# A fused adaLN layer on one core: GpSimd keeps only short operations, the modulation weights come in other tiles, and all engines get a new order

## The chip, the cores and the metric

The kernel runs on one core of a Trainium2 chip. The metric is the device time of one execution in microseconds (us). Five engines work side by side: PE (TensorE, matrix products), DVE (VectorE), ACT (ScalarE), POOL (GpSimd) and SP (SyncE, which here only issues transfers). Each engine runs its own list of instructions strictly in order, and waits for others through semaphores. Transfers are issued by SP and by ACT. What they share are 16 DMA engines.

## The reference, cut to what matters

```python
mod = (silu(c) @ w_mod).reshape(1, 6, 1, 448)   # sa, ca, ga, sb, cb, gb
h = layernorm(x) * (1 + ca) + sa                # x: 2048 x 448
x = x + ga * (attention(h @ wqkv) @ wo)         # 16 heads of 28; each row sees 8 rows, 2 apart
h = layernorm(x) * (1 + cb) + sb
x = x + gb * (silu(h @ w1) @ w2)                # 448 -> 1792 -> 448
```

Inputs and output are bf16.

## The kernel before, in words

The 2048 rows are split by parity (a row attends only rows of its own parity), which leaves 1024 positions of two rows each. Four chunks of 256 positions are normalized and projected; the attention runs over nine units of 2 x 57 positions, the feed-forward over four chunks again.

A chunk of the first half goes through these steps. **Load** of x (`ldx`). **Normalization**: statistics on DVE (`st`, L356 to L358), the inverse root on POOL (`rstd`, L372), the scaled rows `xn` on DVE (L387) or ACT (L385). **Transpose**: for chunk 0 on PE (L446), for the others by a DMA transpose that SP issues (L404). **Modulation**: scale and shift by columns of `modc` (`mod`, L238 on DVE, L236 on ACT). **Projection** to q and k on PE (`qk`, L473, four pairs of 14 matmuls a chunk) and, by unit, to v (L490). A unit then has logits (`lg`, L528), two exponentials on ACT (`ex`, L535), a mask product on DVE (`mk`, L586), the product with v (`av`, L602), the division on DVE (`rc` and `on`, L609 and L614), a DMA transpose back (`otr`, L617) and a copy to its place (`al`, L623). The output projection (`wo`, L653) follows, then the residual (`res`, L661) and the second normalization, and the feed-forward: L682, silu on ACT (L687), L707 and, for the last rows, L719.

The gates ga and gb are multiplied into the weights wo and w2 (`wog`, L782; `w2g`, L784), once they have been computed on PE (`ga`, `gb`, L335) from the modulation weights `wmod`. `wmod` shares its tile, `both`, with the hidden layer. The columns of sa, ca, sb and cb come from 32 small matmuls each (L317, `mod1`, `mod2`). Before any of it, PE runs matmuls on a tile of zeros (L293, "junk"), and the qk weights are spread out to 32 columns a head on their way to the tile `wp` (`pad`, L432).

Most PE work comes in **pairs**: a first half (`.S`), and a second half (`.C`) that may begin only when POOL, in its own order, has run an empty instruction that waits for the first (`signal`, L218). So whatever stands ahead of that instruction on POOL holds up PE.

Nothing is scheduled at run time. The table `ORDER` lists all 640 steps by number with a letter for the engine (p PE, a ACT, v DVE, g POOL, s SP); each engine's list is what the table has for it. The four double banks of PSUM (`ps`) and the other buffers are handed out in the same order. Each transfer, whoever issues it, takes one of eight completion semaphores in turn (DMAHW0 to 7), and waits until the transfer that had it before has landed.

## Time and profile before

| | |
|---|---|
| median of 3 runs | 189.6 us (187.68 to 190.51) |
| profiled execution, its own time | 186.92 us |
| its span, first to last instruction | 185.1 us |
| mean granted TensorE clock in it | 0.979 of full speed |
| busy: PE, DVE, ACT, POOL | 162.3, 93.7, 96.2, 44.7 us |
| first matmul of the qk projection that is followed by the others without a stop | 14.65 us |
| first matmul of the second chunk pair's projection (chunk 2) | 45.66 us |
| first feed-forward matmul | 81.75 us |
| last matmul of the feed-forward | ends at 176.46 us |

An engine that is busy for its whole span bounds the kernel; one that is not may still hold up another that waits for a certain instruction of it. So the span is read in stretches, and within a stretch by what PE waited for.

### The profile page before, as it was taken

To read this page: it belongs to the slowest core of one execution; us is meant where nothing else is said; L and a number is where in the kernel's file an instruction comes from. 1 tells how busy PE (TensorE), PEld (TensorE's weight loads), DVE (VectorE), ACT (ScalarE), POOL (GpSimd) and SP (SyncE) were. 2 spreads that over 40 slices of the span, in tenths; PEclk is the share of its full clock that TensorE was granted. 3 is DMA by queue.
4 is the path that set the end of the run, shared out by engine and by line. 5 is a ranking of instruction groups with operands and counts; after the bars stand their busy time and mean duration, and the time that the engine had idled before them with its cause. 6 is when DMAs were issued, how large, how long until landed. Compare 5 with 4: busy or idle time off the path is not lost.

```text
span 185.1 us, 6152 instructions
## 1 busy us (share of the span) xinstructions
PE 162.3 (88%) x2713; PEld 84.8 (46%) x2713; DVE 93.7 (51%) x194; ACT 96.2 (52%) x128; POOL 44.7 (24%) x91
## 2 busy tenths in 40 slices
PE   7979799677868989879999999999999999999910
PEld 2344354354334545545556644455444445554700
DVE  2879999679557858993327484032062000002620
ACT  2140598725259657586698785585338854200000
POOL 6346434551100059432304202000400000000000
PEclk9999999997899999999999999999999999999995
DMA  5993599999687956434003343900009000000132
GB/s 176 339 360 84 96 200 239 110 132 119 210 62 197 212 199 31 89 75 102 0 0 60 64 104 68 109 0 4 0 3 259 4 0 4 0 0 4 50 102 66
DMA packets 33114, 18.20 MB, mean 98 GB/s; under 512 B 25016, under 2 KB 32568, under 8 KB 33080
## 3 DMA queue, kind: packets, MB, share of 16 engines
q1 hardware_dynamic: 30752, 14.92, 40.7%
q10 hardware_dynamic: 2328, 2.81, 4.9%
q8 instruction: 23, 0.38, 0.9%
q14 instruction: 11, 0.09, 0.2%
HBM read 9.86 MB, written 1.84 MB: 63 GB/s over the span
## 4 chain that ended last, share of the span: by engine, by line
PE 70%; DVE 8%; DMA 6%; POOL 5%; ACT 3%; issue 2%; DVEq 0%; POOLq 0%; ACTq 0%
PE ps L682 23%; PE ps L707 20%; PE ps L473 10%; PE ps L653 5%; DMA wqk<-in_A_wqkv_dram 4%; PE ps L490 4%; PE ps L719 3%; PE ps L602 2%; PE ps L528 2%; POOL rs L372 2%; DMA x_all<-in_A_x_dram 2%; DVE xn L387 1%; ACT ho L236 1%; DVE st L356 1%; DVE p L586 1%
## 5 line engine op out<-in xcount | busy, mean ns | idle before, releaser
L707 PE MATMUL ps<-w,both 64*128 64x448 bf16 x392 | 38.9, 349 | 0.0
L687 ACT ACTIVATE both<-ps 128x1024 bf16<-128x1024 f32 x28 | 27.8, 1022 | 17.6 <-PE ps L682 17.2
L473 PE MATMUL ps<-ho,wp 64*128 64x512 bf16 x224 | 26.9, 385 | 3.9 <-POOL ho L623 1.4
L682 PEld LDWEIGHTS <-w 64*128 64x128 bf16 x392 | 20.0, 94 | 22.5 <-issue 1.0
L707 PEld LDWEIGHTS <-both 64*128 64x128 bf16 x392 | 19.0, 94 | 17.6
L682 PE MATMUL ps<-h,w 64*128 64x512 bf16 x196 | 22.5, 376 | 0.6 <-ACT v L495 0.6
L682 PE MATMUL ps<-wqk,w 64*128 64x512 bf16 x196 | 22.3, 376 | 0.0
L661 DVE SCALAR_TENSOR_TENSOR x_all<-ps,x_all 128x448 bf16<-128x448 f32 x16 | 9.3, 621 | 22.6 <-PE ps L653 22.6
L473 PEld LDWEIGHTS <-wp 64*128 64x128 bf16 x224 | 11.3, 95 | 17.3 <-issue 3.8
L535 ACT ACTIVATE p<-ps 128x912 bf16<-128x912 f32 x18 | 15.9, 929 | 5.4 <-PE ps L528 5.3
L742 DVE TENSOR_TENSOR wqk<-ps,x_all 128x896 bf16<-128x896 f32 x3 | 3.3, 1087 | 26.8 <-issue 26.8
L490 PE MATMUL ps<-wv,ho 64*64 64x448 bf16 x252 | 14.8, 352 | 1.8 <-issue 1.4
L477 ACT CAST qk<-ps 128x1024 bf16<-128x1024 f32 x11 | 10.5, 1016 | 7.9 <-PE ps L473 7.9
L387 DVE TENSOR_SCALAR xn<-x_all,mv,rs 128x512 bf16<-128x512 bf16 x26 | 12.4, 509 | 4.2 <-POOL rs L372 4.2
L364 POOL TENSOR_SCALAR mv<-sums 128x2 f32<-128x2 f32 x8 | 3.0, 376 | 41.8 <-DVE x_all L661 34.3
L653 PE MATMUL ps<-wo,ho 64*128 64x448 bf16 x112 | 12.8, 350 | 0.0
L367 ACT ACTIVATE scr<-x_all,mv 128x448 bf16<-128x448 bf16 x16 | 10.6, 664 | 3.8 <-POOL mv L364 3.5
L586 DVE TENSOR_TENSOR p<-p,maskb 128x1824 bf16<-128x1824 bf16 x9 | 11.7, 1299 | 1.7 <-ACT p L535 1.7
L356 DVE BATCH_NORM_STATS2 st<-x_all 128x6 f32<-128x448 bf16 x16 | 9.9, 619 | 2.7 <-DMA x_all<-in_A_x_dram 2.7
L614 DVE TENSOR_TENSOR o<-ps,rc 121x896 bf16<-121x896 f32 x9 | 9.8, 1086 | 0.7 <-DMA op<-o 0.5
L490 PEld LDWEIGHTS <-ho 64*64 64x64 bf16 x252 | 7.1, 106 | 6.5 <-issue 4.0
L293 PE MATMUL ps<-junk 64*128 64x512 bf16 x56 | 9.0, 488 | 1.2 <-DVE junk L203 1.2
(84 smaller groups left out, 175.7 us busy)
## 6 DMA issues: line engine op xcount, KB each, us to landing
w<-in_B_w_dram SPq DMA_DIRECT2D x2, 896.0 KB, 6.0
w<-in_B_w_dram SPq DMA_DIRECT2D x2, 784.0 KB, 5.9
x_all<-in_A_x_dram SPq DMA_DIRECT2D x2, 448.0 KB, 10.0
out_dram<-ot SPq DMA_DIRECT2D x4, 224.0 KB, 2.2
both<-in_w_mod_dram ACTq DMA_DIRECT2D x1, 784.0 KB, 8.5
wo<-in_A_wo_dram SPq DMA_DIRECT2D x2, 392.0 KB, 6.0
both<-in_w_mod_dram SPq DMA_DIRECT2D x1, 784.0 KB, 9.3
out_dram<-wqk SPq DMA_DIRECT2D x3, 224.0 KB, 2.3
```

What stands on the lines that cost most here:

```text
L356: V.bn_stats(out=st[:], in_=x_all[:, us[t], :])
L367: S.activation(out=scr[:], in_=x_all[:, us[t], :], func=ACTF.Square, bias=mv[:, t, 0:1], accum_out=mv[:, t, 1:2])
L387: (V if o["eng"] == "dve" else G).tensor_scalar(out=out_, in0=in_, scalar1=mv[:, t, 0:1], scalar2=rs[:, t:t + 1], op0=ALU.subtract if b el ...
L473: return [matmul(t[:, j, :], lhsT=w, rhs=hT[rows, :, kt, s0:s0 + CP], start=start, stop=stop)]
L477: copy_on(o)(out=qk[:, :, g, :, s0:s0 + CP], in_=t[:].rearrange("p j (t s) -> p j t s", t=2))
L490: return [matmul(t[half(par), j, 0:D], lhsT=hT[rows, par, kt, k0:k0 + KB], rhs=wv[rows, kt, :], start=start, stop=stop) for par in range(2)]
L535: S.activation(out=p_of[u][:, 2 * t * w:2 * t * w + 2 * w].rearrange("p (j n) -> p j n", j=2), in_=bank(a, t)[:, :, 0:w], func=ACTF.Exp, s ...
L586: V.tensor_tensor(out=p, in0=p, in1=m, op=ALU.mult)
L653: x = matmul(t[:, par, 0:D], lhsT=oT[rows, par, i // 2, 128 * m:128 * m + 128], rhs=wo[rows, j, :], start=(j == 0), stop=(j == 5))
L682: return [matmul(t[:, i // 7, :], lhsT=w1[rows, kt, 128 * i:128 * i + 128], rhs=h[rows, :, kt, :], start=start, stop=stop)]
L687: S.activation(out=hid[:, k % 2, :, i, :], in_=t[:], func=ACTF.Silu)
L707: x = matmul(t[:, par, 0:D], lhsT=hid[half(hf), k % 2, jj, ii, 128 * j:128 * j + 128], rhs=w2[half(hf), ii + 7 * jj, :], start=(way == 0 a ...
```

## The change

It does five things. (1) Modulation weights: the 448 rows of `w_mod` were four tiles of 112 rows; they are now rows 0, 128, 256 in steps of 128 plus a fourth tile at row 320 that overlaps the third by 64 rows. The entries of silu(c) that belong to the doubled rows are left at zero in one of the two (L303 after, four small matmuls instead of one). Each load becomes two (three tiles, then one). (2) The vectors ga, sb, cb and gb, which were three loads, are one pair of loads. (3) Long POOL work goes elsewhere: two of the four pads, the first gate product on wo, four of the seven on w2 and two alignment copies now may run on DVE (or ACT) only. What stays on POOL is the inverse root, a few 128x2 operations, the fills and the signals. (4) Adding epsilon moves from DVE (16 instructions, L358) into the POOL step of the inverse root (one more 128x2 instruction for eight pairs); `nm`, needed only where ACT normalizes, is left out elsewhere, and `nm` and `mean` may run on DVE as one instruction. (5) `ORDER` is new throughout. By kind, the moves between DVE and ACT are: normalizations on DVE 26 to 20 and on ACT 6 to 12, modulations on DVE 14 to 19 and on ACT 14 to 9, evictions of qk and v on ACT 17 to 19 and on DVE 8 to 6.

```diff
-21g 0s 64v 63v 30p 33p 32p 48p 45p 35p 41p 44p 1a 65g 34p 31p 46p 39p 69v 70v 40p 36p 2a 3a 20a 7a 8a 71g 22g 72g 66g 67v 53a 68v 73v 74v 6s 9s 4s 54p
+23g 30p 21g 34p 27g 36p 40p 0a 64v 63v 1a 3a 2s 8a 20a 69v 70v 53a 54p 55a 6a 9s 33p 4s 41p 44p 7s 65g 29g 37p 49p 52p 35p 66v 67a 71g 72g 112v 111v
...
-    wmod = both[0:KM, 0:KT * 6 * D].rearrange("p (k n) -> p k n", k=KT)
+    wmod = both[:, 0:KT * 6 * D].rearrange("p (k n) -> p k n", k=KT)
...
     def load_mod(name, c0, c1):
-        return dma(name, f"ldm{(c1 - c0) // D}", wmod[:, :, c0:c1], w_mod.rearrange("(k p) n -> p k n", p=KM)[:, :, c0:c1])
+        n = (c1 - c0) // D
+        return [dma(f"{name}0", f"ldm{n}x3", wmod[:, 0:3, c0:c1], w_mod[0:384, c0:c1].rearrange("(k p) n -> p k n", p=128)),
+                dma(f"{name}1", f"ldm{n}x1", wmod[:, 3, c0:c1], w_mod[320:448, c0:c1])]
...
-    ld_mo, ld_mb, ld_m2 = load_mod("ldm_ga", 2 * D, 3 * D), load_mod("ldm_sb", 3 * D, 5 * D), load_mod("ldm_gb", 5 * D, 6 * D)
+    ld_mo = ld_mb = ld_m2 = load_mod("ldm_b", 2 * D, 6 * D)
...
     def c_cols(o):
-        matmul(bank(o)[0:KM, 0, 0:KT], lhsT=sc4[:], rhs=ident[0:KT, 0:KT], start=True, stop=True)
+        for hf, c0, n, at, step in ((0, 0, 3, 0, 2), (0, 8, 1, 3, 1), (1, 1, 3, 0, 2), (1, 6, 1, 3, 1)):
+            matmul(bank(o)[half(hf), 0, at:at + n], lhsT=sc7[:], rhs=ident[0:7, c0:c0 + step * (n - 1) + 1:step], start=True, stop=True)
...
-                V.tensor_scalar(out=mv[:, t, 1:2], in0=mv[:, t, 1:2], scalar1=EPS, scalar2=None, op0=ALU.add)
...
             def rstd(o):
-                if not b:
-                    G.tensor_scalar(out=rs[:], in0=mv[:, :, 1], scalar1=1.0 / D, scalar2=EPS, op0=ALU.mult, op1=ALU.add)
-                G.tensor_tensor(out=rs[:], in0=mv[:, :, 1] if b else rs[:], in1=negh[:], op=ALU.pow)
+                G.tensor_scalar(out=rs[:], in0=mv[:, :, 1], scalar1=1.0 if b else 1.0 / D, scalar2=EPS, op0=ALU.mult, op1=ALU.add)
+                G.tensor_tensor(out=rs[:], in0=rs[:], in1=negh[:], op=ALU.pow)
 
             def shift(o):
+                if all(x["eng"] != "act" for x in self.xn):
+                    return
+                if o["eng"] == "dve":
+                    V.scalar_tensor_tensor(out=nm[:], in0=mv[:, :, 0], scalar=-1.0 if b else 1.0, in1=rs[:], op0=ALU.mult, op1=ALU.mult)
+                    return
...
-    pads = [P.op(f"pad{kt}", "vag", "pad", lambda o, kt=kt: pad(o, kt), [ld_qk[kt // 2]]) for kt in range(KT)]
+    pads = [P.op(f"pad{kt}", "va", "pad", lambda o, kt=kt: pad(o, kt), [ld_qk[kt // 2]]) for kt in range(KT)]
...
-        al_done[u] = P.op(f"al{u}", "vag", "align", align, [trs] + late)
+        al_done[u] = P.op(f"al{u}", "va", "align", align, [trs] + late)
...
-            wo_gated = [P.op(f"wog{i}", "vg", "wog", lambda o, i=i, n=n: eng[o["eng"]].tensor_tensor(out=wo[:, i:i + n], in0=wo[:, i:i + n],
+            wo_gated = [P.op(f"wog{i}", "v", "wog", lambda o, i=i, n=n: eng[o["eng"]].tensor_tensor(out=wo[:, i:i + n], in0=wo[:, i:i + n],
...
-            w2_gated = [P.op(f"w2g{f}", "vg", "w2g", lambda o, f=f: eng[o["eng"]].tensor_tensor(out=w2[:, f:f + 2, :], in0=w2[:, f:f + 2, :],
+            w2_gated = [P.op(f"w2g{f}", "v", "w2g", lambda o, f=f: eng[o["eng"]].tensor_tensor(out=w2[:, f:f + 2, :], in0=w2[:, f:f + 2, :],
```

**Place 1: POOL in the attention.** Before, from the last `nm` of the first half to the second inverse root of the second half (`wo`, `w_76` are the weights that get their gates, `ho<-op` an alignment copy):

```order
L375 TENSOR_TENSOR nm<-mv,rs 128x2
L377 TENSOR_SCALAR nm<-nm 128x2
L782 TENSOR_TENSOR wo<-wo,gbc 128x1792
L623 COPY ho<-op_79 128x8x114
L364 TENSOR_SCALAR mv<-sums 128x2 x2
L371 TENSOR_SCALAR rs<-mv 128x2
L372 TENSOR_TENSOR rs<-rs,negh 128x2
L784 TENSOR_TENSOR w_76<-w_76,gbc 128x896
```

And the same place of the change:

```order
L371 TENSOR_SCALAR rs<-mv 128x2
L372 TENSOR_TENSOR rs<-rs,negh 128x2
L365 TENSOR_SCALAR mv<-sums 128x2
L371 TENSOR_SCALAR rs<-mv 128x2
L372 TENSOR_TENSOR rs<-rs,negh 128x2
L380 TENSOR_TENSOR nm<-mv,rs 128x2
```

No operation on a wide tile is left there; the signals of the pairs (not printed, since they only wait) stand between these rows.

**Place 2: DVE between the divisions of units 0 and 1 and the mask of unit 2.** Before (`ho<-ho` is the modulation of chunk 2, `o0` and `o1` the divided units, `xn` normalized rows of chunk 3, `v3` an eviction):

```order
L609 RECIPROCAL rc_104<-ps0_109 121x32
L614 TENSOR_TENSOR o0_95<-ps0_109,rc_104 121x2x448
L609 RECIPROCAL rc_104<-ps1_110 121x32
L614 TENSOR_TENSOR o1_96<-ps1_110,rc_104 121x2x448
L238 TENSOR_SCALAR ho_77<-ho_77,modc_101 128x2x256
L495 CAST v3_91<-ps2_111 128x32x28
L387 TENSOR_SCALAR xn3_83<-x_all_66,mv_138,rs_139 128x512
```

The change:

```order
L237 TENSOR_SCALAR ho_77<-ho_77,modc_101 128x2x256 x2
L614 RECIPROCAL rc_104<-ps1_110 121x32
L619 TENSOR_TENSOR o0_95<-ps1_110,rc_104 121x2x448
L614 RECIPROCAL rc_104<-ps3_112 121x32
L619 TENSOR_TENSOR o1_96<-ps3_112,rc_104 121x2x448
L237 TENSOR_SCALAR ho_77<-ho_77,modc_101 128x2x256
L392 TENSOR_SCALAR xn2_82<-x_all_66,mv_141,rs_142 128x512
L392 TENSOR_SCALAR xn3_83<-x_all_66,mv_138,rs_139 128x512 x2
L392 TENSOR_SCALAR xn2_82<-x_all_66,mv_141,rs_142 128x512
L787 TENSOR_TENSOR wo_73<-wo_73,gbc_102 128x1792
L787 TENSOR_TENSOR wo_73<-wo_73,gbc_102 128x1344
```

Two of the modulations now stand ahead of the divisions, the v eviction is gone to ACT, and both gate products on wo are here.

**Place 3: the start of ACT, which issues transfers there.** What a row waits for is in brackets. Before:

```order
L241 DMA x_all<-in_A_x_dram 128x896
L241 DMA c_67<-in_c_dram 4x112
L241 DMA both<-in_w_mod_dram 112x4x896
L266 ACT_TABLE_LOAD
L241 DMA wqk<-in_A_wqkv_dram 128x2x896 [waits DMAHW0_49]
L241 DMA x_all<-in_A_x_dram 128x2x896 [waits DMAHW1_49]
L298 ACTIVATE sc_68<-c_67 4x112 [waits DMAHW2_49]
L303 CAST scT<-ps_110 112x4 [waits PE_49]
L241 DMA wv<-in_A_wqkv_dram 128x2x448
L241 DMA both<-in_w_mod_dram 112x4x448 [waits DMAHW3_49]
L432 COPY wp<-wqk 128x32x28
L236 ACTIVATE ho<-ps_111,modc 128x2x128 [waits DVE_49,PE_49]
```

The change:

```order
L240 DMA x_all<-in_A_x_dram 128x896 x2
L240 DMA both<-in_w_mod_dram 128x3x896
L240 DMA wqk<-in_A_wqkv_dram 128x2x896
L267 ACT_TABLE_LOAD
L299 ACTIVATE sc_68<-c7_67 7x64 [waits DMAHW1_49]
L305 CAST scT<-ps_110 128x4 [waits PE_49]
L240 DMA wv<-in_A_wqkv_dram 128x2x448 [waits DMAHW3_49]
L390 ACTIVATE xn_80<-x_all,nm,rs 128x512 [waits DMAHW0_49,DVE_49]
L390 ACTIVATE xn_80<-x_all,nm,rs 128x512
L437 COPY wp<-wqk 128x32x28 [waits DMAHW7_49]
L235 ACTIVATE ho<-ps_112,modc 128x2x128 [waits DVE_49,PE_49]
```

Now the second half of the qk weights (`wqk`) is issued without a wait, behind both halves of x's first chunk and three quarters of the modulation weights; the pad on that half of the weights (DMAHW7) stands ahead of the modulations of chunk 0. SP issues c, x of chunk 1, the last quarter of the modulation weights and the first half of the qk weights at once, and the rest of x behind them.

## Rows read from the trace of the kernel before

**Rows 1.** Windows: stretch us, busy (count) PE PEld DVE ACT POOL, clock, DMA share, GB/s.

```profile
0.00:14.65 14.65, 11.82 (x111) 5.38 (x113) 9.30 (x30) 3.70 (x6) 7.66 (x26) 1.00 0.92 292
14.65:45.65 31.00, 25.13 (x642) 13.43 (x642) 27.55 (x64) 18.29 (x21) 14.77 (x27) 0.97 0.86 135
45.65:81.75 36.10, 30.57 (x815) 16.68 (x807) 27.33 (x40) 22.75 (x32) 12.44 (x14) 0.98 0.69 140
81.75:176.50 94.75, 94.72 (x1154) 49.31 (x1154) 28.26 (x59) 51.45 (x70) 9.86 (x24) 1.00 0.20 41
176.50:185.00 8.50, 0.06 (x2) 0.00 (x0) 1.27 (x4) 0.00 (x0) 0.00 (x0) 0.74 0.30 92
```

**Rows 2.** Timeline, 24 to 56 us: start, us, engine, line, operation, tiles, [idle before, releaser].

```profile
32.26 0.84 POOL L375 TENSOR_TENSOR nm<-mv,rs 128x2 f32<-128x2 f32 x1
32.96 1.05 DVE L387 TENSOR_SCALAR xn<-x_all,mv,rs 128x512 bf16<-128x512 bf16 x3
33.21 1.47 PE L473 MATMUL ps<-ho,wp 64*128 64x512 bf16 x12 [0.89 <-POOLq L218]
38.90 3.57 POOL L782 TENSOR_TENSOR wo<-wo,gbc 128x1792 bf16<-128x1792 bf16 x1 [3.61 <-PE ps L490]
39.42 3.20 DVE L238 TENSOR_SCALAR ho<-ho,modc 128x512 bf16<-128x512 bf16 x1
43.67 1.33 PE L335 MATMUL ps<-both,screp 112*128 112x448 bf16 x4 [1.18 <-DVE v L495]
43.86 0.40 DVE L238 TENSOR_SCALAR ho<-ho,modc 128x512 bf16<-128x512 bf16 x1
51.41 1.69 PE L473 MATMUL ps<-ho,wp 64*128 64x512 bf16 x14 [1.42 <-POOL ho L623]
54.13 2.12 PE L473 MATMUL ps<-ho,wp 64*128 64x512 bf16 x18 [1.04 <-ACT ho L623]
```

**Rows 3.** Groups by line and shape: out<-in xcount | busy us, mean ns | idle.

```profile
L387 DVE TENSOR_SCALAR xn<-x_all,mv,rs 128x512 bf16<-128x512 bf16 x26 | 12.4, 509 | 4.2 <-POOL rs L372 4.2
L784 POOL TENSOR_TENSOR w<-w,gbc 128x896 bf16<-128x896 bf16 x4 | 7.5, 1880 | 0.6 <-PE ps L473 0.6
L238 DVE TENSOR_SCALAR ho<-ho,modc 128x512 bf16<-128x512 bf16 x8 | 5.7, 755 | 0.0
L385 ACT ACTIVATE xn<-x_all,nm,rs 128x512 bf16<-128x512 bf16 x6 | 4.8, 818 | 3.1 <-POOL nm L375 3.1
L358 DVE TENSOR_SCALAR mv<-mv 128x1 f32<-128x1 f32 x16 | 2.5, 154 | 0.6
L784 DVE TENSOR_TENSOR w<-w,gbc 128x896 bf16<-128x896 bf16 x3 | 1.7, 575 | 0.0
```

**Rows 4.** Timeline, 0 to 24 us.

```profile
9.20 0.94 ACT L432 COPY wp<-wqk 128x896 bf16<-128x896 bf16 x1 [0.78 <-issue]
10.44 0.95 PE L317 MATMUL ps<-scT,both 112*128 112x1 bf16 x32 [1.25 <-DMA both<-in_w_mod_dram]
12.52 1.02 ACT L236 ACTIVATE ho<-ps,modc 128x256 bf16<-128x256 bf16 x2 [2.38 <-DVE ho L238]
12.79 1.81 POOL L432 COPY wp<-wqk 128x896 bf16<-128x896 bf16 x2 [2.21 <-DMA wqk<-in_A_wqkv_dram]
23.18 0.70 PE L528 MATMUL ps<-qk 28*64 28x57 bf16 x64 [1.32 <-DVE qk L477]
```

**Rows 5.** Transfers by issue: out<-in, queue, count, KB each, us from issue to landing.

```profile
both<-in_w_mod_dram SPq DMA_DIRECT2D x1, 784.0 KB, 9.3
both<-in_w_mod_dram SPq DMA_DIRECT2D x1, 392.0 KB, 9.8
```

**Rows 6.** Chain of waits in order of time: start us, us, what.

```profile
14.65 5.57 PE ps L473 x50
20.22 1.67 PE ps L490 x32
88.75 1.32 PE ps L653 x14
```

## The prediction

> **What bounds the kernel now.** I read the windows first, cut where PE starts a new kind of work [rows 1]. In the last long stretch, the feed-forward from 81.75 us on, PE is busy 94.72 of 94.75 us: nothing but less PE work could shorten it, and the change takes no PE work away. In the two attention stretches PE is busy 25.13 of 31.00 and 30.57 of 36.10 us. That leaves 5.87 + 5.53 = 11.4 us in which PE waits. The granted clock there is 0.97 and 0.98, so the matmuls themselves ran longer by about 0.03 x 31.0 + 0.02 x 36.1 = 1.6 us. So 13.0 us can be won there, and no more. Before them lies the start (14.65 us), after them a tail of 8.5 us.

> Then the timeline, for what PE waited for in those 13 us. The largest places [rows 2]: 1.42 us for an alignment copy on POOL, 1.18 us for a v eviction on DVE, 1.04 us for a copy on ACT, 0.89 us for a signal on POOL; and 1.32 us for a qk eviction on DVE [rows 4]. No engine is full (DVE 27.55 and 27.33 us of 31.00 and 36.10, ACT 18.29 and 22.75, POOL 14.77 and 12.44 [rows 1]); PE waits because the instruction that it needs stands behind another one. One such pair is plain to see: POOL multiplies wo from 38.90 for 3.57 us; a DVE modulation that starts at 39.42 takes 3.20 us, where the same instruction takes 0.40 at 43.86; the v eviction stands behind it on DVE, and PE loses the 1.18 us. While the long POOL operation runs, DVE as good as stands still.

> **The change, part by part.**

> *Long operations leave POOL.* It loses 3.57 (wo), 7.5 (four times 1.88 on w2) and 1.81 us (two pads) [rows 2, 3, 4], and two alignment copies. DVE gets the products: 575 ns for 896 columns [rows 3], so 1.15 for the 1792 columns of wo and 2.3 for the four on w2, together 3.45 us where POOL took 11.1. The stretching of DVE goes with them: the eight modulations have a mean of 755 ns against 0.40, which is 2.8 us; the 26 normalizations, of the same size, 509 against 0.40, another 2.8 us [rows 2, 3]. The epsilon instructions go, 2.5 us [rows 3]; part of this lies beside the start. DVE also hands six normalizations to ACT (2.4 us) and takes five modulations (2.0 us), some in the feed-forward. Net, DVE gets roughly 5 us lighter over the attention; ACT gets six times 818 ns [rows 3] heavier and sheds five modulations, and has 26 us free there [rows 1]. So neither becomes the bound by its sum.

> *Start.* Chunk 0's projection needs x, all of sa and ca and both halves of the qk weights. These are the first eight transfers now, none waits for a semaphore, and x of chunk 1 is among them: 448 + 448 + 896 + 896 KB, 2.75 MB. At the 292 GB/s of the start [rows 1] that is 9.4 us, a landing near 10.2 us at best. At worst the last half of the qk weights, behind 1120 KB on ACT's queue, lands as late as now, 12.79 [rows 4]. I take 12.6, near the late end, since SP's other loads of x follow at once and share the engines. Then ACT, in its own order, runs a pad (0.94) and four modulation instructions (two take 1.02) before PE can begin: 12.6 + 0.94 + 2.04 = 15.6. Now it is 14.65, where POOL's two pads end after 12.79 + 1.81. **The start costs 1.0 us**; bounds: 0.2 us won (early landing, the modulation vectors 2 us later still on PE at 10.44 and its transposes ahead) and 1.5 lost.

> *To chunk 2's projection.* I followed the new lists by hand, with durations of like rows. Chunk 0 takes 56 x 5.57/50 = 6.2 us on PE, and the first halves of v 1.67 [rows 6]. The eviction that PE waited 1.32 us for now ends beneath those 1.67 us, since DVE has less in front of it. Chunk 1's rows are normalized earlier because their x is among the first eight loads; their transposes and modulations end before PE asks for them. The 0.89 us on a signal goes, as fewer POOL steps stand ahead of it; the 1.18 us goes with the wo product. What could be late next is chunk 2: its two modulations now stand ahead of the divisions of units 0 and 1 on DVE, and wait for transposes that SP issues behind the one big load. That load is 1344 + 448 KB. I let it start near 20 us and land at 27 to 31 (the present pair of 784 and 392 KB took 9.3 and 9.8 us, with other loads beside it [rows 5]); the transposes then land by 32 or 33, when DVE gets there. I leave 0.5 of the 5.87 us standing.

> *To the feed-forward.* The waits of 1.42 and 1.04 us sat on copies that are now elsewhere, but others come. Chunk 3's modulations are waited for on DVE (two us, beneath PE's four pairs of chunk 2). The output projection of the second 128 rows needs unit 2's copy, whose transpose is issued right after its division: about 0.9 us on PE. Logits 5 need a bank that a residual frees: 0.5. With two lesser ones I leave 2.0 of the 5.53 us, and 0.3 of the 1.6 of the clock.

> *Feed-forward and tail.* Two more output projections (1.32 us each [rows 6]) stand ahead of it, which shifts work and adds none. The w2 products lie beneath PE: DVE is busy 28.26 of 94.75 us there. One of three last stores goes to SP, behind the flag: 0, bounds 0.6 either way.

> **Sum.** 13.0 - 0.5 - 2.0 - 0.3 = 10.2 won, 1.0 lost at the start, and 1.2 held back for handovers that a chain by hand leaves out: **8 us faster**. The profiled execution took 186.92 us (span 185.1), 2.7 below the median of 189.6; so 178.9 against the profile, **181.5 against the median**.

> **The rivals.**

> A. *Short POOL operations hold PE instead.* At 32.26 a POOL instruction on 128x2 elements takes 0.84 us while DVE works, and the pair behind it on PE starts 0.89 late [rows 2]. Seven inverse roots or means stand ahead of signals between here and the feed-forward in the new order, each with one POOL instruction more. At 0.89 each that is 6.2 us, and 1.8 are left of the 8: 187.8. For it: DVE's long products are more numerous now. Against: the statistics are ready earlier, and a signal needs POOL only at its own time. [...]

> B. *Slower: the feed-forward is no longer dense.* ACT, with 51.45 of 94.75 us busy there [rows 1], gets normalizations on top, and each of the four chunks needs modulated rows at its start. Earlier arrival of PE there means that statistics, transposes and modulations have less time. If each of the four borders stalls PE by 3 us, 12 are lost: 193.5. It decides from 2.95 us a border on, (8 + 3.8)/4. Against: today's list has 0.03 us of wait there.

> C. *The big load holds the transposes.* If it lands as slowly as the present loads, 1176 KB in about 10 us [rows 5], 1792 KB take 15 us from 20, and chunk 2's transposes land near 37. DVE stands before the divisions, and PE gets chunk 2 some 4 us later: gain 4, 185.5.

> That the change doesn't do what it says is hardly possible: the lists show it.

> **Numbers.** Forecast, 5 to 12 us won: 0.60. C: 0.13. A: 0.17. B: 0.10. What a measurement here can tell from no change is 2%, 3.8 us: below 185.8 is faster. The forecast and most of C lie there, 0.72; A and the rest of C within 2%, 0.19; slower 0.09. The range ends at 188, which takes in A, and at 176, which is the whole 13.0 us won and nothing lost (189.6 - 13.0 = 176.6).

> **What would show it.** Right: PE's first unbroken qk matmul at 15 to 16 us; chunk 2's at 39 to 42 (now 45.65); the first feed-forward matmul at 74 to 78, with two more projections behind it; granted clock near 1.00 throughout; modulations on DVE near 0.40 us each; then 92 us of PE without a gap. Wrong: waits of PE for POOL's sequencer on many pairs (A), idle PE at chunk borders after 80 us (B), DVE waiting for the transposes of chunk 2 (C).

## The result, and the profile after

The changed kernel takes **180.28 us** (median of 4 runs, 179.35 to 180.61) beside 188.64 for the kernel before on the same chip (4 runs, 187.11 to 190.51): ratio 0.958, 95% interval 0.950 to 0.966. The forecast was 181.5, with a range of 176 to 188. The profiled execution took 179.35 us with a span of 177.5, so 7.6 us less than the one profiled before. (Ratios and their intervals leave out executions over 1.5% above the shortest of the same kernel, medians do not; the median of the kernel before moved between 186.18 and 188.73 us from one comparison to the next, so an experiment is judged against its own runs of before, and two experiments by their ratios.)

Windows of the changed kernel, cut where PE starts a new kind of work; columns as in [rows 1]:

```profile
0.00:15.51 15.51, 11.14 (x110) 5.02 (x111) 8.86 (x27) 6.15 (x11) 7.67 (x30) 1.00 0.75 267
15.51:42.16 26.65, 24.56 (x552) 13.14 (x553) 20.93 (x47) 18.55 (x22) 6.42 (x14) 0.94 0.70 180
42.16:77.35 35.19, 33.23 (x932) 18.95 (x932) 25.46 (x47) 24.72 (x34) 3.01 (x6) 1.00 0.82 154
77.35:169.70 92.35, 92.06 (x1126) 47.20 (x1126) 28.04 (x62) 51.55 (x71) 6.52 (x18) 1.00 0.18 38
169.70:178.00 8.30, 0.07 (x2) 0.00 (x0) 1.27 (x4) 0.00 (x0) 0.00 (x0) 0.72 0.26 81
```

Against [rows 1], PE's idle time in the two attention stretches fell from 5.87 + 5.53 to 2.09 + 1.96 us: 7.35 won. The third stretch is only 0.9 us shorter, but holds 2.66 us more work, the two output projections that came out of the feed-forward. What the clock costs did not change: 0.94 over 26.65 us is 1.6 us, as much as both stretches together cost before. But its place did. In the kernel before, the low clock stood in the attention, behind two waits close together (1.07 us without a releaser up to 41.05, and the 1.18 us up to 43.67 [rows 2]):

```profile
41.05 0.55 PE L528 MATMUL ps<-qk 28*64 28x57 bf16 x46 [1.07 <-issue]
44.00:47.40 3.40, 3.40 (x76) 1.25 (x73) 2.08 (x6) 2.03 (x3) 0.00 (x0) 0.51 0.80 143
```

In the changed kernel that place runs at 1.00, and the low clock has a new one at the start, shown below.

What PE waited for in the whole execution (line, releaser: us in total, times, longest):

```profile
PE ps L533 <- issue: 2.9, 4, 1.6
PE ps L478 <- ACT ho L235: 2.5, 1, 2.5
PE ps L294 <- DVE junk L202: 1.2, 1, 1.2
PE ps L319 <- DMA both<-in_w_mod_dram: 0.6, 1, 0.6
PE ps L687 <- issue: 0.5, 1, 0.5
PE ps L478 <- DVE ho L628: 0.5, 1, 0.5
PE ps L687 <- ACT h L235: 0.3, 1, 0.3
PE ps L478 <- ACT p L540: 0.2, 1, 0.2
```

The waits of [rows 2] on POOL, on a v eviction and on copies are gone, and so is the 1.32 of [rows 4]. Of waits for other engines inside the attention only 0.5 and 0.2 us are left; the 2.5 us belong to the start. In first place stands "issue": 2.9 us inside the logits (L533), in which PE waited for nothing that the profile shows.

The timeline of the start, answering to [rows 4], shows a second thing:

```profile
11.09 0.94 ACT L437 COPY wp<-wqk 128x896 bf16<-128x896 bf16 x1 [2.83 <-DMA wqk<-in_A_wqkv_dram]
12.98 1.37 DVE L237 TENSOR_SCALAR ho<-ps,modc 128x256 bf16<-128x256 bf16 x4 [1.50 <-ACT ho L235]
14.44 0.56 ACT L235 ACTIVATE ho<-ps,modc 128x256 bf16<-128x256 bf16 x1 [1.50 <-DVE ho L237]
15.06 8.15 PE L478 MATMUL ps<-ho,wp 64*128 64x512 bf16 x56 [2.46 <-ACT ho L235]
```

The weights land at 11.09, 1.7 us earlier than before, but then ACT and DVE, which share the modulations of chunk 0, wait for each other 1.50 us each, and PE stands idle for 2.46. Its first two matmuls come at 15.06, the others without a stop from 15.51 (the mark of the table in "Time and profile before": 14.65 there, with six matmuls ahead of it from 13.74). Behind that idle time the 56 matmuls of chunk 0's projection take 8.15 us where 50 took 5.57 [rows 6]. Windows of that place show why:

```profile
15.06:16.60 1.54, 1.48 (x12) 0.70 (x13) 1.47 (x5) 1.54 (x3) 0.07 (x1) 0.93 0.26 50
16.60:20.00 3.40, 3.40 (x18) 1.45 (x16) 3.26 (x11) 1.89 (x3) 0.83 (x2) 0.53 0.70 173
20.00:23.20 3.20, 3.20 (x34) 1.55 (x34) 0.43 (x2) 1.46 (x3) 1.82 (x5) 1.00 0.86 202
```

For 3.4 us the granted clock is at half (0.53 over the window): 18 matmuls, against 34 in the next 3.2. At the later pace 18 would take 1.7 us, so another 1.7 are lost.

Groups by line and shape, answering to [rows 3] (normalization, modulation, w2 product, all on DVE):

```profile
L392 DVE TENSOR_SCALAR xn<-x_all,mv,rs 128x512 bf16<-128x512 bf16 x20 | 7.4, 404 | 1.9 <-POOL rs L372 1.9
L789 DVE TENSOR_TENSOR w<-w,gbc 128x896 bf16<-128x896 bf16 x7 | 4.2, 617 | 0.0
L237 DVE TENSOR_SCALAR ho<-ho,modc 128x512 bf16<-128x512 bf16 x10 | 3.8, 416 | 3.2 <-DMA ho<-xn 3.2
```

A modulation takes 416 ns on average in place of 755, a normalization 404 in place of 509: the stretching by POOL is gone, as forecast (with the long operations back on POOL, e2 below, the modulations take 560 ns). Whether the 8 us came from that is what the experiments ask.

### The profile page after: what moved, and what is told of

It reads as the page before. It is cut to its first block, busy times and chain, and to the rows that moved or that the text cites. A ratio compares the mean times of both kernels' runs of the same rounds, so it can differ in the third digit from the quotient of the medians.

```text
span 177.5 us, 6130 instructions
## 1 busy us (share of the span) xinstructions
PE 161.1 (91%) x2716; PEld 84.3 (47%) x2716; DVE 84.6 (48%) x186; ACT 101.0 (57%) x136; POOL 23.6 (13%) x68
## 4 chain that ended last, share of the span: by engine, by line
PE 77%; DMA 8%; ACT 5%; DVE 3%; issue 3%; ACTq 1%; DVEq 0%
PE ps L687 24%; PE ps L712 21%; PE ps L478 15%; DMA wqk<-in_A_wqkv_dram 5%; PE ps L658 4%; PE ps L495 4%; PE ps L533 3%; PE ps L724 3%; PE ps L607 3%; DMA h<-xn 3%; ACT p L540 1%; ACT h L235 1%; ACT ho L235 1%; PE ps L337 1%; ACTq L240 1%
## 5 line engine op out<-in xcount | busy, mean ns | idle before, releaser
L712 PE MATMUL ps<-w,both 64*128 64x448 bf16 x392 | 39.2, 349 | 0.0
L687 PEld LDWEIGHTS <-w 64*128 64x128 bf16 x392 | 19.8, 94 | 23.1 <-issue 1.8
L478 PE MATMUL ps<-ho,wp 64*128 64x512 bf16 x224 | 27.6, 395 | 3.2 <-ACT ho L235 2.5
L747 DVE TENSOR_TENSOR ot<-ps,x_all 128x896 bf16<-128x896 f32 x6 | 6.5, 1090 | 38.1 <-issue 20.6
L478 PEld LDWEIGHTS <-wp 64*128 64x128 bf16 x224 | 12.0, 98 | 16.5 <-issue 3.5
L482 ACT CAST qk<-ps 128x1024 bf16<-128x1024 f32 x12 | 11.8, 1014 | 5.4 <-PE ps L478 5.4
L495 PE MATMUL ps<-wv,ho 64*64 64x448 bf16 x252 | 13.7, 352 | 0.0
L591 DVE TENSOR_TENSOR p<-p,maskb 128x1824 bf16<-128x1824 bf16 x9 | 10.1, 1121 | 5.4 <-ACT p L540 5.3
L390 ACT ACTIVATE xn<-x_all,nm,rs 128x512 bf16<-128x512 bf16 x12 | 9.4, 811 | 4.9 <-POOL nm L380 2.7
L658 PE MATMUL ps<-wo,ho 64*128 64x448 bf16 x112 | 12.2, 350 | 0.0
L372 POOL TENSOR_TENSOR rs<-rs,negh 128x2 f32<-128x2 f32 x16 | 11.3, 708 | 1.3
L371 POOL TENSOR_SCALAR rs<-mv 128x2 f32<-128x2 f32 x16 | 3.1, 197 | 56.6 <-ACT scr L368 21.0
L358 DVE BATCH_NORM_STATS2 st<-x_all 128x6 f32<-128x448 bf16 x16 | 9.7, 605 | 1.9 <-DMA x_all<-in_A_x_dram 1.9
```

What stands on the lines that cost most here:

```text
L372: G.tensor_tensor(out=rs[:], in0=rs[:], in1=negh[:], op=ALU.pow)
L478: return [matmul(t[:, j, :], lhsT=w, rhs=hT[rows, :, kt, s0:s0 + CP], start=start, stop=stop)]
L482: copy_on(o)(out=qk[:, :, g, :, s0:s0 + CP], in_=t[:].rearrange("p j (t s) -> p j t s", t=2))
L495: return [matmul(t[half(par), j, 0:D], lhsT=hT[rows, par, kt, k0:k0 + KB], rhs=wv[rows, kt, :], start=start, stop=stop) for par in range(2)]
L591: V.tensor_tensor(out=p, in0=p, in1=m, op=ALU.mult)
L658: x = matmul(t[:, par, 0:D], lhsT=oT[rows, par, i // 2, 128 * m:128 * m + 128], rhs=wo[rows, j, :], start=(j == 0), stop=(j == 5))
```

## The experiments

Names are those of the code: wog0 and w2g* are the products with the gates on wo and w2, al* the alignment copies, pad* the copies of the qk weights, and the letters p, a, v, g, s stand for PE, ACT, DVE, POOL and SP.

**e1 and e5: the kernel before without the long POOL operations.** e1 moves the pads too:

```diff
- wog0 g, w2g0 g, w2g2 g, w2g6 g, w2g10 g, al0 g, al5 g, pad2 g, pad3 g
+ wog0 v, w2g0 v, w2g2 v, w2g6 v, w2g10 v, al0 a, al5 a, pad2 a, pad3 v   (e1)
+ wog0 v, w2g0 v, w2g2 v, w2g6 v, w2g10 v, al0 a, al5 a                   (e5)
```

> The kernel before, its order untouched, with only the engine letters of nine steps changed: the gate product on wo and four on w2 from POOL to DVE, two alignment copies and a pad from POOL to ACT, a pad from POOL to DVE. Theory P (long POOL operations cost time by themselves, through DVE and through the signals behind them): the 1.18 and the 1.42 us of PE's waits go and most of the 1.6 us of the clock, 3 to 5 us faster than before (ratio 0.973 to 0.985). Theory O (the new order did it, POOL is beside the point): within 1 us of before, since DVE and ACT get the work at places that were not made for it.

> The kernel before, with its order untouched and the two pads left on POOL, so that the start is as before (14.65 us); only the long POOL operations of the attention and the feed-forward change engine: the product on wo and four on w2 go to DVE, two alignment copies to ACT. Theory P (the long POOL operations are what costs the 11.4 us of PE's waits, by stretching DVE and by standing in front of signals): the waits of 1.18 and 1.42 us go, the modulations take 0.40 us, and at least 3 us are won, 185.5 or less beside 188.6. Theory O (the order and the loads of the changed kernel win it): other waits take their place, 187.5 to 189.

Measured: e1 187.81 beside 187.92 us, without a ratio, so unclear; e5 185.81 beside 186.18, ratio 0.997 (0.990 to 1.005). The operations got shorter as they should, in e5:

```profile
L387 DVE TENSOR_SCALAR xn<-x_all,mv,rs 128x512 bf16<-128x512 bf16 x26 | 10.9, 453 | 4.5 <-POOL rs L372 4.5
L238 DVE TENSOR_SCALAR ho<-ho,modc 128x512 bf16<-128x512 bf16 x8 | 2.9, 406 | 0.0
```

And next to nothing came of it in time. PE's waits in e5, the largest of the attention:

```profile
PE ps L528 <- issue: 2.1, 2, 1.1
PE ps L473 <- ACT ho L623: 2.1, 2, 1.0
PE ps L490 <- issue: 1.4, 2, 1.2
PE ps L602 <- issue: 1.1, 1, 1.1
PE ps L528 <- DVE qk L477: 0.9, 1, 0.9
PE ps L473 <- POOLq L218: 0.9, 1, 0.9
```

The 1.42 us on POOL's copy [rows 2] became 1.05 on ACT's; the 1.18 on a v eviction is gone; and "issue" is 4.6 us, where the kernel before had 2.6. What PE no longer waits for on DVE, it waits for with no releaser (what that is, e7, e9 and e12 show). Theory P falls as the cause of the gain in the old order: at most 1.0% by the interval, where it asked for 1.6% and more. One thing blurs this test. In e5's traced execution the unbroken projection starts at 15.56 and not at 14.65, behind half clock from 12.4 to 15.8 us (0.57 over 12 to 16), which its edit does not touch; from there to the first feed-forward matmul e5 takes 66.1 us, the kernel before 67.1. So the operations may be worth about 1 us in the attention. In e1 the start comes at 16.56.

**e2: the changed kernel with the long operations back on POOL** (the pads stay off).

```diff
- wog0 v, w2g0 v, w2g2 v, w2g6 v, w2g10 v, al0 a, al5 a
+ wog0 g, w2g0 g, w2g2 g, w2g6 g, w2g10 g, al0 g, al5 g
```

> The changed kernel, its order untouched, with the gate product on wo, four on w2 and the two alignment copies back on POOL. Theory P: it loses 3 to 6 us of the 8 (183 to 186 us). Theory O: it loses under 1.5 us (below 182).

Measured: 180.98 us (180.74 to 181.34), ratio to before 0.974 (0.960 to 0.989). By the ratios that is 1.6% (3 us) slower than the changed kernel, with as much uncertainty; by the medians, of different comparisons, 0.7 us. So the time does not separate P from O. The traces speak for O: wo takes 4.3 us on POOL, yet PE's waits, added over the same table as above, grow from 8.7 to 9.5 us only, and the span from 177.5 to 178.8.

**e3 and e6: the tiles of the modulation weights alone.** e3 is the changed kernel with four tiles of 112 rows, its loads cut in the same two pieces; e6 the kernel before with tiles of 128.

```diff
- w_mod[0:384, c0:c1].rearrange("(k p) n -> p k n", p=128)   ... w_mod[320:448, c0:c1]
+ w_mod[0:336, c0:c1].rearrange("(k p) n -> p k n", p=112)   ... w_mod[336:448, c0:c1]   (e3; e6 the other way round)
```

> The changed kernel with modulation weights in four tiles of 112 rows again, same loads, same order. My sum has no term for the tiles: within 1 us of the changed kernel (179.3 to 181.3 us). Rival L (128 rows make the loads shorter and that is part of the gain): 2 us or more slower, with the first modulation matmul later than 8.68 us by over 1 us.

> The kernel before, with one part of the change alone: the modulation weights as four overlapping tiles of 128 rows (each of the three loads in two pieces, on the queue where the load was), everything else in its old order. Before, the chip moved 310 to 330 GB/s between 7 and 11 us with tiles of 112 rows, after it 380 with 128. Theory T (the wider tiles make the start's loads faster): 300 to 385 GB/s there, the last half of the qk weights lands about 1.5 us earlier than 12.79, and the first unbroken qk matmul comes at 13.0 to 13.8 in place of 14.65; the kernel 1 us faster, 187.5 against 188.6, if the later waits stay as they are. Rival: the rate is set by the engines and not by the rows; the extra 112 KB cost 0.3 us, the start is at 14.7 to 15.0 and the time 188.6 to 189.

Measured: e3 182.65 us (180.12 to 183.04), ratio 0.975 (0.938 to 1.013), which separates it neither from the changed kernel nor from before; e6 186.37 beside 186.18, ratio 1.002 (0.995 to 1.008). The rate is real: from 7 to 11 us it is 319 to 324 GB/s in the four traces with tiles of 112 rows (before, e1, e5, e3) and 368 to 394 in the ten with 128. The transfers of the kernel before and of the changed one in that stretch, and (7 to 9 us, by windows) of e3:

```profile
DMA packets 880, 1.29 MB, mean 321 GB/s; under 512 B 37, under 2 KB 880, under 8 KB 880
```
```profile
DMA packets 999, 1.52 MB, mean 381 GB/s; under 512 B 56, under 2 KB 999, under 8 KB 999
```
```profile
7.00:9.00 2.00, 0.60 (x6) 0.10 (x2) 1.93 (x8) 1.52 (x2) 1.30 (x4) 1.00 1.07 292
```

What the rate is worth is another matter. In e3 the pads could start at 12.87, in the changed kernel at 11.09, but e11 below, with the start and the tiles of the changed kernel, has 12.17. And in e6, at 385 GB/s, the last half of the qk weights lands at 12.57 (before: 12.79) and the unbroken projection starts at 14.43 (before: 14.65): theory T had 1.5 us and 13.0 to 13.8, so it fails at the start already, and the rival's 14.7 to 15.0 is nearer. So far as single executions show, neither part gives the early landing alone: 12.57 with the tiles in the old order, 12.87 with the new order and 112 rows, 11.09 to 12.17 with both (the changed kernel, e2, e11). In the attention PE idles 10.35 us in e6 in place of 11.4, but the wait for the v eviction ahead of the second gate is 2.00 us long (1.18 before), and the clock is at half for 6.8 us behind it (0.50 over 44 to 48 us, 0.72 over 48 to 52; 3.4 us before), which takes the rest back.

**e10: both parts in the old order** (e5 and e6 together).

> The kernel before with both named parts of the change except the new order: the modulation weights as tiles of 128 rows (as in e6) and the long operations off POOL (as in e5, pads kept), every engine's list otherwise as before. Theory O (the order of the engines and loads wins the 8 us): 185 to 187 beside 186 to 188.6, PE's waits for POOLq, for ACT ho L623 and for instructions still there, ratio 0.98 to 1.00. Theory B (the two parts are worth nothing alone, but together free the chain): waits of PE in the attention fall below 7 us, ratio 0.97 or less.

Measured: 185.29 beside 188.73 us, ratio 0.983 (0.973 to 0.992). This is between the theories: 1.75%, 3.3 us, where each part alone gave nothing that could be measured (at most 1.0% and 0.5% by their intervals). PE's largest waits in the attention keep the pattern of the old order:

```profile
PE ps L533 <- issue: 2.2, 2, 1.9
PE ps L478 <- ACT ho L628: 2.1, 2, 1.0
PE ps L478 <- POOLq L221: 1.2, 1, 1.2
PE ps L533 <- DVE qk L482: 0.7, 1, 0.7
```

The changed kernel stands at 0.958 (0.950 to 0.966): what the rest of the change adds to both parts is about 2.5% of 188, 4.7 us, with roughly 2.4 us of uncertainty (both intervals together). That rest is the new order of engines and loads, and with it the two pads off POOL, the epsilon instructions and the joint load, which no run takes apart. None of the three rows here that are not "issue" is left in the changed kernel's table.

**e11: two output projections put back behind the feed-forward's first pairs**, with their additions on DVE.

```diff
- PE: ... av6 wo3.S wo4.S wo3.C wo2.S wo4.C wo2.C f100.S f105.S f100.C f105.C f106.S
+ PE: ... av6 wo2.S wo2.C f100.S f105.S f100.C f105.C wo3.S wo4.S wo3.C wo4.C f106.S
```

> The changed kernel with two output projections (rows 384 to 511 and 512 to 639, 1.32 us each on PE) put back behind the first two pairs of the feed-forward, as the kernel before has them, their additions on DVE with them. Theory W (part of the gain: these 2.65 us fill time in which PE would wait for the transposes and modulations of the feed-forward's first chunk, which come at 77 us): PE idles some 2 to 2.6 us more before the first feed-forward matmul, which stays at 76 to 77.5, the dense stretch is 94.7 us in place of 92.1, and the kernel takes 182.3 to 183 beside 180.3. Rival V (the order only moves work): the feed-forward starts at 74.7, dense for 94.7: 180.3.

Measured: 184.11 us, but 180.19 to 185.93 and no ratio, so the time is unclear. The traced execution, the longest of the four (185.93), speaks for W. With a start 1.08 us late (16.14 for 15.06) the first feed-forward matmul still comes only at 77.35, and PE waits twice for the modulations:

```profile
73.93 1.79 PE L658 MATMUL ps<-wo,ho 64*128 64x448 bf16 x14
77.35 0.39 PE L687 MATMUL ps<-h,w 64*128 64x512 bf16 x2 [1.63 <-ACT h L235]
78.76 5.73 PE L687 MATMUL ps<-h,w 64*128 64x512 bf16 x26 [1.02 <-ACT h L235]
```

The changed kernel has 0.8 us there (0.52 and 0.29). So in this execution the moved work leaves a wait of 1.8 us more, and the last 26 matmuls run 5.73 us, at a lower clock behind the idle time (0.74 over 76 to 80 us). But the shortest execution took 180.19 us, which is what V forecasts, and it has no trace; so how much of the gain of the changed kernel comes from work that fills a wait stays open.

**e4: another start.** The changed kernel with all modulations of chunk 0 on DVE, right behind the vectors they need, and all pads on ACT:

```diff
- v: mod1.ev pad3 h00.mod1 h01.mod1 pad0 pad1        a: n10.xn1 pad2 h00.mod0 h01.mod0
+ v: mod1.ev h00.mod0 h00.mod1 h01.mod0 h01.mod1     a: n10.xn1 pad0 pad1 pad3 pad2
```

> The changed kernel with a new start: the eight modulation instructions of chunk 0 all on DVE, ahead of the pads, and the four pads on ACT as their weights land. In the changed kernel DVE and ACT wait for each other there (1.50 us twice), PE's projection starts at 15.06 to 15.5 us after 2.5 us of idling and then runs 3.4 us at half clock. If those are the cost: projection from about 13.0 us, no half clock behind it, 2 to 4 us faster than the changed kernel (176.3 to 178.3 us). Rival (absorbed): the chunk 2 transposes, instruction issue and the wait at the feed-forward's start take it back, under 1 us faster.

Measured: **177.38 us** (176.81 to 177.91), ratio to before 0.955 (0.939 to 0.970). It is the lowest median of all kernels here, but by its ratio it is not separated from the changed kernel (0.958); profile against profile its span is 2.0 us shorter. In the timeline of PE:

```profile
14.02 5.79 PE L478 MATMUL ps<-ho,wp 64*128 64x512 bf16 x52 [1.12 <-ACT wp L437]
25.25 0.60 PE L533 MATMUL ps<-qk 28*64 28x57 bf16 x51
28.01 0.32 PE L533 MATMUL ps<-qk 28*64 28x57 bf16 x13 [2.15 <-issue]
```

The unbroken projection starts at 14.02 in place of 15.51 and runs at full clock (1.00 from 14 to 20 us). But a gap of 2.15 us has come after 51 of the 64 matmuls of the second logits, without a releaser (0.36 there in the changed kernel), and the half clock now stands behind it (0.60 from 28.3 to 31.7 us).

**e7, e9, e12: what the gaps are.** The transfers have a queue of the kind "instruction", with 23 pieces of 16 KB over the changed kernel's execution, about 250 PE instructions (2716 matmuls and as many weight loads, 5432 in all) for each but the last; in e4 one starts at 25.5 us, as a load of 1792 KB ends. The three kernels are e4 with loads moved on SP (n*.tr are transposes, ldm_b0 and ldm_b1 the second modulation load, ldwo0 and ldw10 halves of wo and w1):

```diff
- s: ldx3 n13.tr n12.tr ldm_b0 ldm_b1 n14.tr n15.tr ldw10 ldwo0 n17.tr n16.tr otr1   (e4)
+ s: ldx3 ldm_b0 ldm_b1 n13.tr n12.tr n14.tr n15.tr ldw10 ldwo0 n17.tr n16.tr otr1   (e7)
+ s: ldx3 n13.tr n12.tr n14.tr n15.tr ldm_b0 ldm_b1 ldwo0 n17.tr n16.tr otr1         (e9; ldw10 on ACT behind v2.ev)
+ s: ldx3 n13.tr n12.tr ldm_b0 n14.tr n15.tr ldm_b1 ldwo0 n17.tr n16.tr ldw10 otr1   (e12)
```

> e4 with one thing moved on SP: the two pieces of the second modulation load (1792 KB) right behind the load of x of chunk 3, ahead of the first two transposes, so that they follow the start's loads at once and are over near 18.5 us, not between 20 and 25. In e4 PE stops for 2.15 us after the 51st of the 64 matmuls of the second logits (25.85 to 28.01), and its next 16 KB of instructions are fetched at 25.5, as the load ends; half clock for 3.4 us comes behind. Theory F (the load holds back PE's instruction fetch, which would be due near 21.7 us): the fetch comes before 23 us, the 2.15 us and the half clock behind it (1.7 us) go: 173.5 to 174.5 beside 177.4. Rival N (small matmuls simply run through their instructions faster than these can be fetched, whatever the loads do): the gap stays after the same 51 matmuls and as long; 177 to 178. Rival Q: the transposes of chunk 1, now behind the load on the same queue, land some 2 us later and chunk 1 starts late: 178 to 180.

> e4 with its later loads moved into times when PE has just been given instructions. [...] Here the second modulation load (1792 KB) and the second half of wo go on SP behind the transposes of chunk 1's other half, near 25 us, and the first half of w1 goes on ACT's queue behind the last v eviction before the gates, near 37 us. Theory F (loads hold back the fetch): the second fetch comes near 22 us, no gap in the second logits, no gap in the third, and no half clock after 14 us: 173.0 to 174.5 beside 177.4 for e4, against before about 0.933. Rival N (small matmuls outrun the fetch whatever the loads do): a gap of about 2 us stays inside the second or third logits, ratio 0.954 as e4.

> e4 with the second modulation load split in time, on SP alone: its first piece (1344 KB) stays where it was, near 18 us, so that it is over by 22; the second piece (448 KB) and the half of wo come behind the transposes of chunk 1's other half, near 28, and the first half of w1 behind those of chunk 2, near 39. Theory F (PE's instructions are fetched only when the loads in flight are done): the fetch that came at 25.5 in e4 comes at 22 to 23, the gap of 2.15 us in the second logits and the half clock behind it go, the third logits have no gap; 173.5 to 175 beside 177.4, ratio to before 0.93 to 0.945. Rival G (the gap only moves on: the next load meets the next fetch, as in e7): the second logits are whole, but 1 to 2 us of gaps come in the third or fourth, 176.5 to 178, ratio 0.95 to 0.955. Rival N (small matmuls outrun the fetch whatever the loads do): the gap stays in the second logits after the same 51 matmuls, 177.4.

Measured: e7 178.04 us beside 186.18 (ratio 0.957, 0.949 to 0.964), e9 180.39 beside 188.73 (0.958, 0.953 to 0.964), e12 179.55 beside 186.84 (0.961, 0.956 to 0.966). By these ratios none is separated from e4 or from the changed kernel. But the gap in the second logits behaves as theory F says:

| | PE begins the first logits | transfers end near | piece fetched at | that is, behind the first logits' begin | gap in the second logits |
|---|---|---|---|---|---|
| e9 | 23.0 | none under way | 24.0 | 1.0 | 0 |
| e7 | 23.1 | 23 | 24.3 | 1.2 | 0 |
| e12 | 21.4 | 24.6 | 24.7 | 3.3 | 1.20 |
| e4 | 21.4 | 25.0 | 25.5 | 4.1 | 2.15 |

The same 64 matmuls in e7 and in e12:

```profile
27.04 0.70 PE L533 MATMUL ps<-qk 28*64 28x57 bf16 x64
```
```profile
25.32 0.59 PE L533 MATMUL ps<-qk 28*64 28x57 bf16 x51
27.11 0.26 PE L533 MATMUL ps<-qk 28*64 28x57 bf16 x13 [1.20 <-issue]
```

And the rates from 14 to 30 us in slices of 0.4 us, e4 first, then e9, whose 41 near 24 us is the piece alone:

```profile
GB/s 188 152 101 67 18 0 35 284 289 48 186 290 180 90 54 81 206 403 385 421 403 412 394 412 421 412 367 128 59 0 0 0 166 290 200 27 282 290 57 166
```
```profile
GB/s 105 309 354 123 25 16 3 253 289 110 0 0 0 0 159 290 206 0 0 0 0 0 0 0 0 41 0 0 0 0 20 0 0 0 0 0 161 204 0 2
```

PE is 1.7 us later in e7 and e9 than in the other two, so the piece must be set against PE's own progress. Behind a load it comes 3.3 and 4.1 us after the first logits have begun, without one 1.0 and 1.2: the load costs it 2.1 to 3.1 us, and PE, which uses up 128 instructions in the 0.7 us of one logits and asks for the 52nd matmul of the second logits 4.5 us after the first ones began, runs dry. For e4 this puts the undisturbed piece near 22.5 (an estimate, 21.4 + 1.0 to 1.2); my 21.7 (expected of e7, and near 22 of e9) was an estimate that no run shows, and 0.8 us early.

That the pieces are PE's and that the gaps are their lateness, the traces show twice. Count PE's instructions (matmuls, weight loads and 20 others) in the 13 traces without e8: each of the 43 waits under "issue" in the attention begins after 193 of them plus a multiple of 256. And in the changed kernel PE goes on 1.2 to 1.5 us after the piece under way has arrived, in all four gaps inside the logits. So e5's 4.6 us of "issue" are waits for instructions too.

Rival N falls for these logits: the same matmuls, in the same order, run without a gap when no load is in the way. It does not fall everywhere. In a later logits (67.62 in the changed kernel) PE stops for 0.16 to 0.91 us in all eight kernels with the new order.

The third logits of the changed kernel (gap 1.57) have the same answer, by e4, whose PE is at nearly the same place at the same time. From 35 to 37 us the changed kernel loads w1 and wo at 370 GB/s, and its piece comes at 39.15; e4 moves 11 GB/s, and its piece comes at 36.09. The two windows and what follows, the changed kernel first:

```profile
35.00:37.00 2.00, 2.00 (x156) 1.70 (x148) 1.13 (x3) 1.38 (x2) 0.19 (x1) 1.00 0.99 370
41.55 0.61 PE L533 MATMUL ps<-qk 28*64 28x57 bf16 x54 [1.57 <-issue]
```
```profile
35.00:37.00 2.00, 2.00 (x150) 1.66 (x140) 1.34 (x2) 1.12 (x2) 0.38 (x2) 1.00 0.04 11
39.48 0.70 PE L533 MATMUL ps<-qk 28*64 28x57 bf16 x64
```

The time was lost again elsewhere each time. e7: the modulation vectors wait 1.56 us for their weights and half clock follows at the start (0.64 over 12 to 16 us; e9, e11 and e12, without the early load, have waits of 2.74, 1.64 and 1.18 there, so the early load need not be the cause), and the third logits have a gap of 1.67 (rival G of e12). e9: SP waits in the transposes until 31 us, so the load lands late and the gates wait 3.6 us for it; the place I gave it, 25 us, was wrong. e12: the third and fourth logits are whole, but the w1 load now stands in front of the transposes of units 0 and 1; the second alignment copy on ACT waits for its transpose, the eviction behind it is late, and PE pays for it (its row, then the window behind it):

```profile
49.94 0.95 ACT L628 COPY ho<-op 128x912 bf16<-128x912 bf16 x1 [1.41 <-DMA op<-o]
```
```profile
51.85 1.68 PE L658 MATMUL ps<-wo,ho 64*128 64x448 bf16 x8 [2.47 <-ACT qk L482]
```
```profile
51.85:55.30 3.45, 3.45 (x80) 1.60 (x81) 2.15 (x4) 1.80 (x3) 0.00 (x0) 0.50 0.19 41
```

**e8: the same question on the changed kernel's third logits.**

```diff
- s: n15.tr ldw10 ldwo0 n17.tr n16.tr otr1 otr0 ldw21
+ s: n15.tr ldwo0 n17.tr n16.tr otr1 otr0 ldw10 ldw21
```

> The changed kernel with one load moved on SP: the first half of w1 (896 KB) behind the transposes of units 0 and 1, so that it starts near 46 us and not at 33. In the changed kernel PE stops for 1.57 us inside the third logits (39.98 to 41.55), its instructions are fetched at 39.2, 436 instructions after the fetch before, and the loads of w1 and wo run from 34 to 39. Theory F (the load holds back the fetch): fetched at about 36, the 1.57 us go, chunk 2's projection starts at 40.6 in place of 42.16, and the kernel gains 1 to 2 us, 178.3 to 179.3, unless the load now holds a later fetch. Rival N (small matmuls outrun the fetch by themselves): the gap stays where it is, 180.3.

Measured: 184.01 beside 186.18 us, ratio 0.981 (0.970 to 0.992): by the ratios slower than the changed kernel, which neither theory expected. The ratio rests on two executions (181.23 and 183.67 us), and the profiled one took 276 us at a clock of 0.56 and shows nothing of the gap. Inconclusive.

## Why the prediction was right, and where it was not

**The time** (forecast 8.0 us won, profile against profile 7.6). The forecast's sum was 13.0 - 0.5 - 2.0 - 0.3 - 1.0 - 1.2. Measured: idle time left 2.09 (0.5 forecast) and 1.96 (2.0); the clock 1.6 (0.3); the start 0.86 by the windows (1.0); the feed-forward 0.26 more idle (0). That leaves 13.0 - 2.09 - 1.96 - 1.6 - 0.86 - 0.26 = 6.2; the tail is 0.8 shorter (7.8 to the span's end in place of 8.6), and PE's busy time behind the start is 0.6 less. So two terms were mis-sized, the stretch to chunk 2's projection by 1.6 and the clock by 1.3 us, and the reserve of 1.2, the tail and PE's 0.6 cover them. The total is right partly by that compensation, which is luck. (189.6 - 8.0 is 181.6; the forecast wrote 181.5.)

**The start.** Forecast 15.6, measured 15.51, by parts that both missed: the weights landed at 11.09 and not at 12.6, and the handover between ACT and DVE ate nearly all of it. The slip was to count ACT's pad and its four modulation instructions, and not DVE's four (1.38 us) that stand between them. The early landing is not a fixed figure either: 12.17 in e11 with the same start.

**The clock.** The step "0.3 of the 1.6" failed, though half of its reason holds. The low clock of the kernel before (44.0 to 47.4) did vanish with the waits ahead of it. But I gave no price to a new wait: the 2.46 us that the new start made were followed by another 3.4 us at half clock (0.53). e4, without that wait, runs chunk 0 at full clock (1.00 from 14 to 20 us).

**Long operations leave POOL.** The step was right in its durations (755 to 416 ns, 509 to 404) and wrong in its worth: I laid the waits of 1.18, 1.42 and 0.89 us at POOL's door. e5 takes the operations away and gains 0.3% (-0.5 to 1.0), e10 with the tiles 1.75% (0.8 to 2.7). DVE did lose beside POOL's product on wo (3.20 us beside 0.40 [rows 2]); but in the old order PE finds the next wait at once, part of it for its own instructions.

**What the order does.** Chunk 2's projection at 42.16 (forecast 39 to 42), the first feed-forward matmul at 77.35 (74 to 78), with two more projections ahead of it: as forecast. The forecast called them work that is shifted and adds nothing; e11's trace has 1.8 us of waiting where they are moved back, its shortest execution none that the time shows, so this stays open. The waits named as late next (unit 2's copy 0.9, a bank for logits 5) did not come. In their place stood gaps that the forecast did not know, 0.36 and 1.57 us of the 2.09 in the first stretch: PE's instructions.

**The rivals.** A fell: no wait on POOL's sequencer is left, and POOL is busy 23.6 us in place of 44.7. B fell: 0.29 us of wait in the feed-forward. C fell as it was put: the big load took 6.6 and 7.0 us, not 15. Its sign did appear, since DVE waited 1.42 us for chunk 2's transposes (to 34.32), but PE had other work meanwhile and lost nothing by it. And C had a point elsewhere: loads held up PE's instructions, by 2.1 to 3.1 us in e12 and e4.

**Open.** Which part of the order is worth what was not taken apart, nor the pads, the epsilon and the joint load from it. The gap in the fourth logits of the changed kernel (0.76 us) is a wait for instructions too, but only transposes are in flight there (up to 297 GB/s in slices of 0.1 us), and e8, which was to test the loads in the changed kernel itself, failed to show anything.

## What to carry to other kernels

A wait that is taken away is only worth what the next one lets through: price a change by undoing it in the new order and doing it alone in the old one, and then do the parts together, since two parts that measured as nothing alone came to 1.75% (0.8 to 2.7) together here (e10). Do not split a short chain between two engines ahead of PE's first work: here that left PE idle for 2.46 us, and the half clock behind it cost 1.7 more. Watch the place of big loads against phases of many small matmuls: the instructions of these came 2 to 3 us late here while such a load ran (e12, e4).
